# Pooled attention with a SwiGLU layer on one Trainium2 core: 68 instead of 30 products of zeros in the first tile

## The chip, the cores and the metric

The kernel runs on one core of one Trainium2 chip. The metric is the device time of one execution in microseconds (us); less is better. Before the change the median of three runs is 977.51 us (976.91 to 977.65).

## What is computed

```python
k_p = k.reshape(B, H, Sp, pool, D).mean(axis=3)        # B=8, H=8, S=576, D=64, pool=8, Sp=72
v_p = v.reshape(B, H, Sp, pool, D).mean(axis=3)
scores = scale * np.matmul(q, k_p.transpose(0, 1, 3, 2))
scores = scores - np.max(scores, axis=-1, keepdims=True)
attn = np.exp(scores)
attn = attn / (np.sum(attn, axis=-1, keepdims=True) + 1e-09)
attn_out = np.matmul(attn, v_p)
x = attn_out.transpose(0, 2, 1, 3).reshape(B * S, H * D)   # 4608 tokens x 512
g = x @ w_gate                                             # d_ff = 1536
silu = g * (1.0 / (1.0 + np.exp(-g)))
out = (silu * (x @ w_val)) @ w_out
```

## The kernel before, in words

The 4608 tokens are cut into nine tiles of 512. A tile is filled by pieces of up to 128 tokens, each of which goes through the attention, and then runs through twelve chunks of 128 hidden columns: a gate product and a value product on TensorE (`side`, L797 to L799, three f16 products for each of four blocks of x), a tanh on ScalarE, two products on VectorE, and an output product (`project`, L824, L830 and L831) that is added up in four PSUM banks `acc`.

The first tile has to do more: it loads and splits all the weights, and it makes the pooled keys and values of two batches. Its order of work is written out by hand in the string `ORDER`. `first_tile` (L907) walks it from left to right; each name is a job of the table `jobs` (L992) and a number, and each engine executes its instructions in the order in which the jobs issue them. The tiles behind it are in another loop and are not touched.

The names used below, with the number of a piece of tokens or a weight chunk or a step of the first tile:

- `H`, `P`, `T` take the weights of a piece of attention into two f16 halves (ScalarE L600, GpSimd L606) and turn them with a transposing DMA (`pt<-half`, SyncE L637); `Y` is its product with the values (TensorE L646 to L649, 16 products); `X` (ScalarE L669) and `Z` (VectorE L673) write the piece into the x of the tile.
- `Lw` loads a weight chunk; `c` (ScalarE L218), `b` (ScalarE L212), `d` (VectorE L222), `e` (ScalarE L233), `f` (TensorE L181 and L182, sums over the partitions), `g` (VectorE L187), `h`, `j` (ScalarE L248), `i`, `k` (VectorE L253) split it into halves.
- `G` and `V` are the gate and the value product of a step (for steps 0 to 5 half a tile, 256 tokens: 12 products each); `t` is its tanh (ScalarE L807), `u` and `v` its products (VectorE L810 and L815), `w` (ScalarE L969) and `y` (VectorE L973) its two halves, `O` the output product (12 products: L824 four times, L830 and L831 four times each).
- `ZERO` begins the four banks `acc` with a product of zeros each (L937). `D` with a number n issues n more products of zeros (L941), each of 512 columns, and adds them to the first bank:

```python
        def idle(n):
            for _ in range(n):
                nc.tensor.matmul(kept["acc"][0], zeros[:, :P], zeros, start=False, stop=False)
```

They add nothing to the result. Steps 0 to 2 work on the first 256 tokens (pieces 0 and 1), steps 3 to 5 on the others (pieces 2 and 3), so `G3` needs `X3` and `Z3`. `G1` writes the bank from which `u0` reads.

Of the kernel before, what the change touches and what calls it, by code (L numbers as in the profile page):

```python
# [37 lines left out]
Lk0 Lq0 Lk1 Lv2 Lv1 Lv0 Lq1 Lw0 Kp0 Kb0 Kp1 CZ Lw1 Lr0 Lu0 S0 Vp0 M0 Lq2 Vp2 E0 Na0 S1  # L38
a0 N0 b0 Vp1 Lq3 M1 Vm0 a1 Vo0 E1 Vs0 Kq0 R0 Vx0 H0 Vh0 Vq0 b1 Vg0 S2 Lr1 Na1 Lu2 P0 S3
Lq4 Vf0 M2 N1 T0 Lq5 H1 Kq1 Vq2 E2 c0 Y0 Lu1 Na2 X0 d0 Z0 Lw2 P1 l0 Vq1 e0 M3 T1 m0 f0  # L40
c1 N2 g0 ZERO Vm1 h0 Vo1 E3 d1 H2 j0 Vs1 Lw3 P2 e1 R1 D10 Y1 Vg1 Vx1 T2 a2 X1 l1 Vh1 un0
b2 m1 Z1 D8 f1 g1 k0 S4 i0 a3 G0 h1 Lq6 j1 M4 un1 c2 V0 k1 t0 Y2 E4 d2 b3 Lw4 i1 Na3 u0
l2 N3 D8 G1 v0 X2 w0 c3 y0 m2 Z2 O0 t1 d3 H3 V1 e2 u1 Lw5 P3 v1 l3 f2 g2 e3 T3 a4 h2 f3
j2 g3 un2 i2 w1 j3 y1 h3 k2 D4 O1 b4 i3 G2 k3 a5 V2 b5 t2 Y3 c4 u2 m3 X3 v2 Vf1 Z3 d4 G3
w2 c5 y2 Lw6 un3 t3 O2 l4 d5 e4 V3 u3 Lw7 m4 l5 f4 G4 v3 g4 w3 m5 y3 j4 O3 e5 k4 V4 Na4
t4 c6 u4 N4 f5 G5 v4 g5 h4 w4 a6 S5 H4 y4 t5 un5 b6 i4 V5 Lq7 u5 P4 M5 O4 G6 v5 T4 un4
a7 w5 c7 y5 d6 E5 O5 t6 j5 u6 Lw8 S6 e6 k5 Na5 V6 h5 Lq8 M6 l6 N5 H5 i5 f6 G7 v6 E6 P5
g6 w6 h6 y6 j6 T5 a8 O6 t7 u7 un6 Na6 c8 S7 b8 b7 V7 M7 i6 G8 E7 v7 d7 w7 Y4 y7 Lw9 N6
e7 O7 t8 d8 H6 X4 u8 Lw10 m6 Y5 e8 Z4 V8 l8 k6 X5 m8 l7 Z5 c9 f7 f8 v8 m7 G9 g7 w8 g8 j7
un7 y8 j8 un8 a9 h7 V9 t9 Na7 b9 u9 N7 O8 v9 i7 k7 w9 H7 y9 G10 k8 c10 d9 h8 V10 t10  # L50
Lw11 i8 e9 u10 La0 a10 l9 f9 O9 v10 m9 g9 w10 h9 y10 j9 un9 O10 i9 b10 k9 La1 a11 G11
b11 d10 V11 t11 Pa0 l10 u11 e10 G12 v11 w11 y11 c11 m10 f10 O11 g10 t12 d11 h10 j10 u12
l11 un10 V12 k10 e11 i10 m11 La2 G13 v12 P6 w12 y12 f11 O12 t13 g11 P7 T6 u13 h11 j11 T7
k11 S8 Ln i11 un11 Pa2 V13 M8 La3 E8 G14 La4 Na8 v13 N8 w13 y13 Y6 Pa3 t14 u14 V14 X6
Pa4 H8 La5 P8 O13 v14 La6 w14 T8 y14 Z6 Pa5 Y7 Pa6 Y8 X7 Z7 X8 La7 Pa1 Z8 Pa7 A A
"""
SIGN_AS_INT = (5, 8, 11)
TILE = 512
# [1085 lines left out]
```

## Time and profile before

| what | value |
|---|---|
| median of the runs | 977.51 us (976.91 to 977.65) |
| the profiled execution, its own time | 975.54 us |
| its span in the trace | 973.8 us |
| TensorE busy | 939.7 us, 97% of the span |
| VectorE, ScalarE, GpSimd busy | 566.0, 461.2, 241.3 us |
| mean granted clock of TensorE | 0.993 |
| products of zeros by `D` (L941) | 30 |

The span runs from the first to the last instruction of the trace; the time of the same execution is 1.74 us longer. "Busy" of TensorE counts the time in which a product is under way. The granted clock is 1.00 at 2.4 GHz and 0.50 at 1.2 GHz. A row of the timeline may hold several instructions of the same line (x8); the bracket behind it says how long the engine had been idle ahead of it, and what ended that.

### The profile page before, as it was taken

The page shows a single profiled execution, that of the slowest core. Times are in us where ns is not written, and L with a number is a line of the kernel's source. Part 1 is how long each engine was busy: PE and PEld are TensorE (multiplying, and loading weights), DVE is VectorE, ACT ScalarE, POOL GpSimd, SP SyncE. Part 2 cuts the span into 40 slices and gives each one's busy share as a digit, 9 for nine tenths or more (in the row PEclk, how much of TensorE's full clock was granted, in tenths as well). Part 3 has the DMA queues.
Part 4 walks back from the last instruction along what each step waited for, and adds up shares of the span by engine and source line. Part 5 has one row for each costly group of instructions (what it writes and reads, how often), then busy time and mean ns, then how long its engine had stood idle before and what let it go on. Part 6 is the DMA issues. An engine that isn't in the chain of part 4 may idle for free.

```text
span 973.8 us, 14306 instructions
## 1 busy us (share of the span) xinstructions
PE 939.7 (97%) x5486; PEld 498.4 (51%) x5486; DVE 566.0 (58%) x1005; ACT 461.2 (47%) x864; POOL 241.3 (25%) x327
## 2 busy tenths in 40 slices
PE   5779999799999999999999999999999999999998
PEld 4657545354555555554555555554545555444443
DVE  6788877667766675586446675674444454323222
ACT  3898883245554553544254544552454443222222
POOL 4533336035226230521025211620121201000000
PEclk9899999999999999999999999999999999999999
DMA  9855426246437342653047232840231222001001
GB/s 349 237 154 208 154 109 171 80 115 186 92 109 211 102 83 79 187 127 82 13 88 235 57 70 87 251 86 15 77 83 43 71 66 55 11 1 44 0 1 44
DMA packets 155524, 103.02 MB, mean 106 GB/s; under 512 B 113216, under 2 KB 141888, under 8 KB 153920
## 3 DMA queue, kind: packets, MB, share of 16 engines
q1 hardware_dynamic: 155456, 102.11, 37.3%
q8 instruction: 43, 0.70, 0.3%
q14 instruction: 25, 0.20, 0.1%
HBM read 67.63 MB, written 9.44 MB: 79 GB/s over the span
## 4 chain that ended last, share of the span: by engine, by line
PE 87%; DMA 6%; POOL 2%; ACT 2%; issue 1%; DVE 1%; SPq 0%; POOLq 0%; DVEq 0%; ACTq 0%
PE gv L797 18%; PE gv L798 18%; PE gv L799 18%; PE acc L824 10%; PE acc L830 9%; PE acc L831 9%; DMA pt<-half 2%; DMA kr<-k_rows 1%; DMA in<-v_rest 1%; DMA in<-k_rows 1%; PE ps L542 1%; PE ps L658 1%; PE ps L543 1%; PE ps L659 1%; DMA k<-k_rows 1%
## 5 line engine op out<-in xcount | busy, mean ns | idle before, releaser
L797 PE MATMUL gv<-x,wgv_h 128*128 128x512 f16 (+1 forms) x888 | 332.0, 374 | 3.8 <-ACT x L669 1.8
L798 PE MATMUL gv<-x,wgv_h 128*128 128x512 f16 (+1 forms) x888 | 331.8, 374 | 1.3 <-DVE x L673 1.3
L799 PE MATMUL gv<-x,wgv_l 128*128 128x512 f16 (+1 forms) x888 | 331.9, 374 | 0.5 <-DVE wgv_l L253 0.5
L810 DVE SCALAR_TENSOR_TENSOR hf<-hf,gv 128x512 f32<-128x512 f32 (+1 forms) x111 | 74.1, 668 | 171.6 <-ACT hf L807 171.3
L807 ACT ACTIVATE hf<-gv,un 128x512 f32<-128x512 f32 (+1 forms) x111 | 74.8, 674 | 193.9 <-PE gv L799 193.9
L1076 ACT CAST hh<-gv 128x512 fp32r<-128x512 f32 x96 | 56.3, 586 | 227.2 <-DVE gv L815 227.2
L831 PE MATMUL acc<-hb,wo_l 128*128 128x512 bf16 x384 | 145.5, 379 | 0.0
L824 PE MATMUL acc<-hh,wo_h 128*128 128x512 f32 (+1 forms) x444 | 139.5, 436 | 0.0
L799 PEld LDWEIGHTS <-wgv_l 128*128 128x128 f16 x888 | 87.0, 98 | 102.2 <-issue 1.7
L798 PEld LDWEIGHTS <-wgv_h 128*128 128x128 f16 x888 | 87.0, 98 | 98.1 <-issue 4.7
L797 PEld LDWEIGHTS <-wgv_h 128*128 128x128 f16 x888 | 87.4, 98 | 94.3
L1080 DVE TENSOR_TENSOR hl<-gv,hh 128x512 bf16<-128x512 f32 x96 | 66.3, 691 | 111.0 <-ACT hb L1077 111.0
L525 POOL TENSOR_TENSOR box<-qt,box 64x512 f16<-64x512 f32 (+1 forms) x60 | 64.0, 1067 | 227.8 <-issue 160.9
L815 DVE SCALAR_TENSOR_TENSOR gv<-gv,un,hf 128x512 f32<-128x512 f32 (+1 forms) x111 | 82.3, 741 | 63.0 <-PE gv L799 62.3
L830 PE MATMUL acc<-hl,wo_b 128*128 128x512 bf16 x288 | 109.8, 381 | 0.0
L824 PEld LDWEIGHTS acc<-hh,wo_h 128*128 128x128 f32 x444 | 83.2, 191 | 24.2 <-ACT hh L969 0.3
L630 POOL TENSOR_TENSOR half<-sc,half 128x512 f16<-128x512 f32 (+1 forms) x30 | 34.7, 1158 | 215.8 <-ACT half L620 193.6
L831 PEld LDWEIGHTS <-wo_l 128*128 128x128 bf16 x444 | 43.7, 98 | 37.9
L1077 ACT CAST hb<-gv 128x512 bf16<-128x512 f32 x96 | 56.8, 591 | 0.0
L830 PE MATMUL acc<-hl,wo_h 128*128 128x512 bf16 (+1 forms) x156 | 56.7, 368 | 0.0
L830 PEld LDWEIGHTS <-wo_b 128*128 128x128 bf16 x288 | 28.3, 98 | 42.2 <-issue 16.6
L523 ACT ACTIVATE qt<-qt,inv 128x512 f32<-128x512 f32 (+1 forms) x60 | 40.9, 682 | 0.0
(143 smaller groups left out, 1121.5 us busy)
## 6 DMA issues: line engine op xcount, KB each, us to landing
ws<-w_all SPq DMA_DIRECT2D x12, 1536.0 KB, 7.1
qt<-q_twice SPq DMA_DIRECT2D x48, 256.0 KB, 3.2
out_t<-ob SPq DMA_DIRECT2D x36, 256.0 KB, 2.3
in<-k_rows SPq DMA_DIRECT2D x12, 576.0 KB, 3.9
in<-q_rows SPq DMA_DIRECT2D x12, 576.0 KB, 5.2
in<-v_main SPq DMA_DIRECT2D x12, 512.0 KB, 4.3
in<-v_rest SPq DMA_DIRECT2D x12, 512.0 KB, 5.7
qt<-q_rows SPq DMA_DIRECT2D x8, 256.0 KB, 4.3
```

Source lines behind the costliest of these rows:

```text
L525: nc.gpsimd.tensor_sub(o[rows], qt[rows], o[rows])
L797: nc.tensor.matmul(o, wh, x["h"][:, j, a:e], start=(j == 0), stop=False)
L798: nc.tensor.matmul(o, wh, x["l"][:, j, a:e], start=False, stop=False)
L799: nc.tensor.matmul(o, wl, x["h"][:, j, a:e], start=False, stop=(j == NJ - 1))
L807: nc.scalar.activation(hf, gate, AF.Tanh, scale=un[:, c, 0:1])
L810: nc.vector.scalar_tensor_tensor(out=hf, in0=hf, scalar=1.0, in1=gate, op0=ALU.add, op1=ALU.mult)
L815: nc.vector.scalar_tensor_tensor(out=out, in0=val, scalar=un[:, c, 2:3], in1=hf, op0=ALU.mult, op1=ALU.mult)
L824: nc.tensor.matmul(o, wo_h[:, c, js], hh[:, :n], start=begin, stop=False)
L830: nc.tensor.matmul(o, wo[:, c, js], hl[:, :n], start=False, stop=False)
L831: nc.tensor.matmul(o, wo_l[:, c, js], hb[:, :n], start=False, stop=end)
L1077: nc.scalar.copy(hb[:, :n], val)
L1080: nc.vector.tensor_sub(hl[:, :n], val, hh[:, :n].bitcast(F32))
```

## The change

Only the string `ORDER` changes. The four `D` that stand there get larger or stay, and four are new. In the order of the program:

| place | before | after |
|---|---|---|
| ahead of `Y1` | 10 | 14 |
| behind `Y1`, ahead of `f1` | 8 | 9 |
| behind `Y2`, ahead of `G1` | 8 | 16 |
| behind `O0`, ahead of `V1` | none | 5 |
| behind `V1`, ahead of `f2` | none | 5 |
| between `f2` and `f3` | none | 6 |
| behind `f3`, ahead of `O1` | 4 | 4 |
| behind `O1`, ahead of `G2` | none | 9 |
| sum | 30 | 68 |

The core of the diff (the lines behind it are the same jobs, broken otherwise):

```diff
-c1 N2 g0 ZERO Vm1 h0 Vo1 E3 d1 H2 j0 Vs1 Lw3 P2 e1 R1 D10 Y1 Vg1 Vx1 T2 a2 X1 l1 Vh1 un0
-b2 m1 Z1 D8 f1 g1 k0 S4 i0 a3 G0 h1 Lq6 j1 M4 un1 c2 V0 k1 t0 Y2 E4 d2 b3 Lw4 i1 Na3 u0
-l2 N3 D8 G1 v0 X2 w0 c3 y0 m2 Z2 O0 t1 d3 H3 V1 e2 u1 Lw5 P3 v1 l3 f2 g2 e3 T3 a4 h2 f3
-j2 g3 un2 i2 w1 j3 y1 h3 k2 D4 O1 b4 i3 G2 k3 a5 V2 b5 t2 Y3 c4 u2 m3 X3 v2 Vf1 Z3 d4 G3
+c1 N2 g0 ZERO Vm1 h0 Vo1 E3 d1 H2 j0 Vs1 Lw3 P2 e1 R1 D14 Y1 Vg1 Vx1 T2 a2 X1 l1 Vh1 un0
+b2 m1 Z1 D9 f1 g1 k0 S4 i0 a3 G0 h1 Lq6 j1 M4 un1 c2 V0 k1 t0 Y2 E4 d2 b3 Lw4 i1 Na3 u0
+l2 N3 D16 G1 v0 X2 w0 c3 y0 m2 Z2 O0 t1 d3 H3 D5 V1 e2 u1 Lw5 P3 v1 l3 D5 f2 g2 e3 T3 a4
+h2 D6 f3 j2 g3 un2 i2 w1 j3 y1 h3 k2 D4 O1 b4 i3 D9 G2 k3 a5 V2 b5 t2 Y3 c4 u2 m3 X3 v2
+Vf1 Z3 d4 G3
```

On TensorE, behind `V1`, where the sums `f2` and `f3` (`ps<-least` and `ps<-wm`, the sums of two weight chunks) stand, the instructions were these; all line numbers of the changed kernel are one higher.

```order
L799 MATMUL gv_643<-x,wgv_l 128x256
L181 MATMUL ps<-least,ones 128x2
L182 MATMUL ps<-wm,ones 128x2
L181 MATMUL ps<-least,ones 128x2
L182 MATMUL ps<-wm,ones 128x2
L941 LDWEIGHTS zeros
L941 MATMUL acc_407<-zeros 128x512
```

And now at the same place:

```order
L800 MATMUL gv_661<-x,wgv_l 128x256
L942 LDWEIGHTS zeros
L942 MATMUL acc_407<-zeros 128x512
...
L182 MATMUL ps<-least,ones 128x2
L183 MATMUL ps<-wm,ones 128x2
L942 LDWEIGHTS zeros
L942 MATMUL acc_407<-zeros 128x512
...
L182 MATMUL ps<-least,ones 128x2
L183 MATMUL ps<-wm,ones 128x2
L942 LDWEIGHTS zeros
L942 MATMUL acc_407<-zeros 128x512
```

Five products of zeros now precede the first sum and six the second. On the other four engines and their queues every instruction stands where it stood.

## Rows read from the trace of the kernel before

**Rows 1.** The page, section 2: granted clock in 40 slices of the span.
```profile
PEclk9899999999999999999999999999999999999999
```

**Rows 2.** Windows: length, busy us of PE, PEld, DVE, ACT, POOL, clock, DMA, GB/s.
```profile
42.87:46.28 3.41, 3.41 (x21) 2.19 (x20) 1.54 (x3) 1.73 (x3) 0.46 (x1) 0.50 1.13 363
63.35:66.74 3.39, 3.39 (x13) 2.22 (x14) 2.94 (x7) 3.39 (x6) 1.87 (x3) 0.50 0.94 329
73.59:77.00 3.41, 3.41 (x18) 2.65 (x17) 3.22 (x3) 3.22 (x6) 0.34 (x1) 0.50 0.33 86
77.00:166.00 89.00, 88.85 (x555) 51.35 (x554) 71.12 (x117) 66.72 (x110) 40.51 (x51) 1.00 0.48 162
```

**Rows 3.** The chain that ended last, pieces in order of time (start, us, what).
```profile
34.02 8.66 DMA pt<-half
62.13 8.50 DMA pt<-half
143.09 0.24 PE ps L182 x2
```

**Rows 4.** Timeline of TensorE, first tile, from the zeros ahead of Y1.
```profile
37.69 2.32 PE L941 MATMUL acc<-zeros 128*128 128x512 f16 x10
...
42.73 0.23 PE L646 MATMUL ps<-pt,vst_h 128*128 128x128 f16 x1 [2.71 <-DMA pt<-half]
...
44.31 2.87 PE L941 MATMUL acc<-zeros 128*128 128x512 f16 x8
```

**Rows 5.** Timeline of ScalarE: X1, w0, X3, t3, the last instruction of e4.
```profile
44.55 0.69 ACT L669 ACTIVATE x<-ps,r 128x512 f16<-128x512 f32 x1 [1.90 <-PE ps L649]
...
57.16 0.35 ACT L969 CAST hh<-gv 128x256 fp32r<-128x256 f32 x1
...
71.77 0.69 ACT L669 ACTIVATE x<-ps,r 128x512 f16<-128x512 f32 x1 [0.57 <-PE ps L649]
...
75.60 0.48 ACT L807 ACTIVATE hf<-gv,un 128x256 f32<-128x256 f32 x1 [0.19 <-PE gv L799]
...
77.62 0.19 ACT L233 ACTIVATION_READ_ACCUMULATOR wgv_h<-wf 128x1 f32 x1
```

**Rows 6.** Timeline of VectorE: g1 and u0.
```profile
47.55 0.16 DVE L187 TENSOR_SCALAR p2w<-ps 128x2 uint32<-128x2 uint32 x1 [1.53 <-PE ps L182]
...
55.88 0.37 DVE L810 SCALAR_TENSOR_TENSOR hf<-hf,gv 128x256 f32<-128x256 f32 x1
```

**Rows 7.** Timeline of TensorE, from the zeros ahead of G1 to G4.
```profile
52.61 1.89 PE L941 MATMUL acc<-zeros 128*128 128x512 f16 x8
56.30 0.27 PE L797 MATMUL gv<-x,wgv_h 128*128 128x256 f16 x1 [1.80 <-ACT ws L212]
...
57.57 0.74 PE L824 MATMUL acc<-hh,wo_h 128*128 128x256 f32 x4
...
59.06 0.27 PE L797 MATMUL gv<-x,wgv_h 128*128 128x256 f16 x1
...
60.37 0.28 PE L181 MATMUL ps<-least,ones 128*128 128x2 f32 x2
61.48 0.38 PE L182 MATMUL ps<-wm,ones 128*128 128x2 f32 x2 [0.83 <-ACT wgv_h L233]
...
63.23 0.50 PE L182 MATMUL ps<-wm,ones 128*128 128x2 f32 x2 [1.14 <-ACT wgv_h L233]
63.59 1.87 PE L941 MATMUL acc<-zeros 128*128 128x512 f16 x4
...
67.33 0.27 PE L797 MATMUL gv<-x,wgv_h 128*128 128x256 f16 x1
...
70.67 0.22 PE L646 MATMUL ps<-pt,vst_h 128*128 128x128 f16 x1 [0.55 <-DMA pt<-half]
...
73.30 0.27 PE L798 MATMUL gv<-x,wgv_h 128*128 128x256 f16 x1 [0.52 <-DVE x L673]
...
78.95 0.36 PE L182 MATMUL ps<-wm,ones 128*128 128x2 f32 x2
```

More of the change, by code (lines that the diff above doesn't have):

```diff
@@ L40 @@
 Lq4 Vf0 M2 N1 T0 Lq5 H1 Kq1 Vq2 E2 c0 Y0 Lu1 Na2 X0 d0 Z0 Lw2 P1 l0 Vq1 e0 M3 T1 m0 f0
-c1 N2 g0 ZERO Vm1 h0 Vo1 E3 d1 H2 j0 Vs1 Lw3 P2 e1 R1 D10 Y1 Vg1 Vx1 T2 a2 X1 l1 Vh1 un0
-b2 m1 Z1 D8 f1 g1 k0 S4 i0 a3 G0 h1 Lq6 j1 M4 un1 c2 V0 k1 t0 Y2 E4 d2 b3 Lw4 i1 Na3 u0
-l2 N3 D8 G1 v0 X2 w0 c3 y0 m2 Z2 O0 t1 d3 H3 V1 e2 u1 Lw5 P3 v1 l3 f2 g2 e3 T3 a4 h2 f3
-j2 g3 un2 i2 w1 j3 y1 h3 k2 D4 O1 b4 i3 G2 k3 a5 V2 b5 t2 Y3 c4 u2 m3 X3 v2 Vf1 Z3 d4 G3
-w2 c5 y2 Lw6 un3 t3 O2 l4 d5 e4 V3 u3 Lw7 m4 l5 f4 G4 v3 g4 w3 m5 y3 j4 O3 e5 k4 V4 Na4
@@ L46 @@
[L46 to L55, printed above, removed]
+c1 N2 g0 ZERO Vm1 h0 Vo1 E3 d1 H2 j0 Vs1 Lw3 P2 e1 R1 D14 Y1 Vg1 Vx1 T2 a2 X1 l1 Vh1 un0
+b2 m1 Z1 D9 f1 g1 k0 S4 i0 a3 G0 h1 Lq6 j1 M4 un1 c2 V0 k1 t0 Y2 E4 d2 b3 Lw4 i1 Na3 u0
@@ new lines @@
+l2 N3 D16 G1 v0 X2 w0 c3 y0 m2 Z2 O0 t1 d3 H3 D5 V1 e2 u1 Lw5 P3 v1 l3 D5 f2 g2 e3 T3 a4
+h2 D6 f3 j2 g3 un2 i2 w1 j3 y1 h3 k2 D4 O1 b4 i3 D9 G2 k3 a5 V2 b5 t2 Y3 c4 u2 m3 X3 v2
+Vf1 Z3 d4 G3 w2 c5 y2 Lw6 un3 t3 O2 l4 d5 e4 V3 u3 Lw7 m4 l5 f4 G4 v3 g4 w3 m5 y3 j4 O3
+e5 k4 V4 Na4 t4 c6 u4 N4 f5 G5 v4 g5 h4 w4 a6 S5 H4 y4 t5 un5 b6 i4 V5 Lq7 u5 P4 M5 O4
+G6 v5 T4 un4 a7 w5 c7 y5 d6 E5 O5 t6 j5 u6 Lw8 S6 e6 k5 Na5 V6 h5 Lq8 M6 l6 N5 H5 i5 f6
+G7 v6 E6 P5 g6 w6 h6 y6 j6 T5 a8 O6 t7 u7 un6 Na6 c8 S7 b8 b7 V7 M7 i6 G8 E7 v7 d7 w7 Y4
@@ new lines @@
+y7 Lw9 N6 e7 O7 t8 d8 H6 X4 u8 Lw10 m6 Y5 e8 Z4 V8 l8 k6 X5 m8 l7 Z5 c9 f7 f8 v8 m7 G9
+g7 w8 g8 j7 un7 y8 j8 un8 a9 h7 V9 t9 Na7 b9 u9 N7 O8 v9 i7 k7 w9 H7 y9 G10 k8 c10 d9 h8
+V10 t10 Lw11 i8 e9 u10 La0 a10 l9 f9 O9 v10 m9 g9 w10 h9 y10 j9 un9 O10 i9 b10 k9 La1
+a11 G11 b11 d10 V11 t11 Pa0 l10 u11 e10 G12 v11 w11 y11 c11 m10 f10 O11 g10 t12 d11 h10
+j10 u12 l11 un10 V12 k10 e11 i10 m11 La2 G13 v12 P6 w12 y12 f11 O12 t13 g11 P7 T6 u13
+h11 j11 T7 k11 S8 Ln i11 un11 Pa2 V13 M8 La3 E8 G14 La4 Na8 v13 N8 w13 y13 Y6 Pa3 t14
@@ L56 @@
+u14 V14 X6 Pa4 H8 La5 P8 O13 v14 La6 w14 T8 y14 Z6 Pa5 Y7 Pa6 Y8 X7 Z7 X8 La7 Pa1 Z8 Pa7
+A A
 """
```

## The prediction

> **What bounds the kernel now.** I read the slices of the granted clock first: only the second of 40, from 24 to 49 us, is below 9 tenths [rows 1], so whatever the zeros do for the clock is decided early. The windows give the falls exactly. From 42.87 to 46.28, 63.35 to 66.74 and 73.59 to 77.00 us TensorE is at 0.50 (1.2 GHz), busy without a break; from 77 to 166 us it is at 1.00 and busy 88.85 of 89.00 us [rows 2]. A fourth stretch lies ahead of the first changed place and is left as it is. Ahead of each of the three the engine stood idle: 2.71 us ahead of Y1; 0.83 and 1.14 us at f2 and f3; 0.55, then the waits for X3 and Z3, of which the last was 0.52 us [rows 4, 7].
>
> Then the chain: which of these falls costs time? It runs through the transposing DMA that lands at 42.68 and the one from 62.13 to 70.63 us, and turns into TensorE only after that; at 143.09 it still goes through a weight sum of TensorE [rows 3]. So what happens ahead of 70.67 us counts only through what makes that DMA start, or if TensorE reaches Y3 later than the DMA lands; what happens behind it counts nearly in full. The DMA from 62.13 waits for P3, this for H3 on ScalarE, and from X1 at 44.55 us ScalarE has no wait until 71.2 us (X3 at 71.77 shows the first, 0.57) [rows 5]. ScalarE is therefore what sets the DMA's start, and X1 waited 1.90 us for TensorE's Y1.
>
> One bound holds for all of this: about 0.2% (1.95 us) is what a measurement of this kernel can tell from no change. A half-speed stretch of 3.41 us costs 1.70 us of TensorE work at most.
>
> **The change part by part.** One product of zeros at 2.4 GHz takes 0.216 us, since ten take 2.32 and eight 1.89 us [rows 4, 7]. That makes 38 more = 8.2 us of TensorE; the question is what they lie in.
>
> *D10 to D14.* Four more end 0.86 us later, at 40.87 instead of 40.01, in a wait that ends at 42.73 with the DMA [rows 4]. They cost nothing; the idle stretch shrinks from 2.71 to 1.85 us. Is that enough for the clock? The nearest row on the one side is this place, where the clock fell behind 2.71 us; the nearest on the other is G1, where it stayed at 1.00 behind eight products of zeros and 1.80 us of idle time [rows 7]. 1.85 is close to the second, so I take it that the fall at 42.87 goes. If it does, Y1 takes as long as Y3: 70.67 to 71.77, 1.10 us, against 42.73 to 44.55, 1.82 us [rows 4, 5, 7]. X1 and all of ScalarE behind it come 0.72 us earlier, so P3, and with it the DMA that now starts at 62.13: it would land at 69.9. (On SyncE's queue it stands behind weight loads, which wait for ScalarE's wf of an earlier chunk and so move with it.) If the fall stays, this term is nothing.
>
> *D8 to D9.* At full clock Y1's 16 products are issued by 43.65 and nine products end at 45.6; now eight end at 47.02 [rows 4]. f1 and g1 come 1.4 us earlier (g1 waited 1.53 us for it [rows 6]). VectorE then reaches u0 1.3 us earlier, at 54.6, bounded by ScalarE's wf (c2).
>
> *D8 to D16.* G1 starts when u0 has left its bank: u0 runs from 55.88 for 0.37 us, and G1 starts at 56.30 [rows 6, 7]. (The row names ScalarE, which ended at the same moment.) With 1.4 us gained, sixteen products run from 51.2 to 54.6 us, and G1 can start at about 55.0. The eight more lie in the wait, and cost nothing. O0 waits for w0 on ScalarE, 57.16 + 0.35 [rows 5], 0.72 earlier: 56.86.
>
> *D5, D5, D6, D9.* From O0 on there is hardly a wait left to fill. The work up to Y3 at full clock: O0 1.49 (57.57 to 59.06), V1 1.31 (59.06 to 60.37), two sums at 0.36 as at 78.95, 5 + 5 + 6 + 4 + 9 = 29 products of zeros 6.26, O1 1.49 as O0, G2 and V2 2.62 as twice V1 [rows 7]: 13.9 us. So TensorE comes to Y3 at 56.86 + 13.9 = 70.75 us, 0.08 later than now and 0.8 us later than the DMA. What the early ScalarE gains, these 25 products give back. The sum holds at full clock, which I take as the 20 products around f2 and f3 lie in the two waits (0.83 and 1.14) that precede the fall at 63.35.
>
> *The fall at 73.59.* With D9 TensorE works through from O1 to the end of Y3; the 0.55 us ahead of Y3 are gone, and only the waits for X3 and Z3 are left. The idle time there is at most 1.53 us (X3's start at 71.77 to 73.30 [rows 5, 7]), less than the 1.80 us that G1 stood without harm, so I take it that the clock stays. Behind 73.3 TensorE is what others wait for, so up to 1.70 us come back. ScalarE lets only part of that through: t3 waited just 0.19 us for G3, and f4 on TensorE (78.95) needs e4, whose last instruction ends at 77.81 [rows 5, 7]. With Y3 0.08 late, e4 ends no earlier than 77.7, so f4 can start at 77.8 to 77.9: some 1.0 us gained. Behind 77 us the engine is busy without a break [rows 2], and what follows moves with it.
>
> *Sum.* 0 + 0 + 0 + 0.08 - 1.1 = about -1.0 us, so the profiled execution would take 974.5 instead of 975.54 us. The median of the runs is 1.97 us above that execution; I put the same step on it: **976.5 us**. Between the bounds: if nothing is late at Y3 and ScalarE follows, -0.72 - 1.70 = -2.4; if no clock is gained at all, +2.7 (below).
>
> **The rivals.**
>
> 1. *The gain comes through in full.* The DMA at 69.9 sets Y3, the fall at 73.59 goes, and ScalarE, 0.72 us earlier, follows: -2.4, 975.1 us. For it: two falls did lie on the chain. Against it: my 13.9 us behind O0. It needs one of the terms there to be 0.8 us too long.
>
> 2. *The fall at 42.87 stays.* 1.85 us of idle time is still more than 1.80. Then X1 is as now, the nine products end at 47.2, u0 0.2 us later, G1 at 56.5, O0 at 57.8 and Y3 at 71.7, 1.0 late; the fall at 73.59 is gone, and ScalarE, which starts from the late X3, gives back little over the 1.0: -0.1, 977.4 us, no change.
>
> 3. *The falls lie elsewhere in other executions.* All of the gain hangs on the fall at 73.59, ahead of which the idle stretches (0.55 us and at most 1.53) are shorter than at the other two places; in an execution without it the same edits bring +0.08: 977.6 us. The three runs lie within 0.74 us, less than one such fall, which speaks against much change from one to the next. The Trainium skill (TensorE: Matmul & The Clock Gate, What's actually happening) says that one kernel shows different numbers of products at the lower level from run to run; no row of one profiled execution can show that. By that rule the time is this rival's.
>
> 4. *The other side: products of zeros do not hold the clock, and 25 of them stand on TensorE's path to Y3.* Ten in a row ended at 40.01 and the clock fell 2.9 us later all the same; the four at 63.59 ran at half speed [rows 2, 4, 7]. Then all falls stay: O0 at 57.8, 13.9 us of work and 1.7 us for the fall at 63.35 put Y3 at 73.4, 2.7 late, with the fall behind it unchanged: 980.2 us. It decides from the point where the clock falls near 63 us although 15 products stand ahead of it. Against it: the row at 52.61, where eight products and a wait of 1.80 brought no fall.
>
> That the change doesn't issue what it says is excluded by the order of TensorE above; the other engines' order is the same.
>
> **How the numbers follow.** Forecast 0.40 (976.5 us), rival 1 0.22, rival 2 0.14, rival 3 0.14, rival 4 0.10. Faster by over 0.2% means below 975.55: rival 1 and a trifle of the forecast, 0.23. Slower means above 979.46: rival 4, 0.10. The rest, 0.67, is no difference. The range leaves out rival 4 and the ends of the others: from 974.6 (rival 1 and half a microsecond, about the spread of the three runs) to 978.6 (rival 2 with Y3 1.0 late and nothing given back).
>
> **What would show it.** In the profile after: an idle stretch of about 1.85 us ahead of Y1, and no 0.50 behind it; X1 at 43.8; G1 near 55.0 right behind sixteen products; the transposing DMA issued near 61.4; no wait ahead of Y3, which starts near 70.75; clock 1.00 from 63 to 77 us; f4's last product near 77.9. Wrong would be: a wait of TensorE for the DMA at Y3 (then rival 1), a fall behind 42.9 (2), any fall between 63 and 77 (4), or a first tile that is 1 us shorter with the gap around 166 to 185 us that much longer.

## The result, and the profile after

The changed kernel takes 981.02 us at the median (977.68 to 982.17, five runs), the kernel before 977.51 us (976.16 to 979.72, five runs in the same session). The ratio is 1.0041 with a 95% interval of [1.0023, 1.0058]: slower by 0.4%. (The ratio is estimated from all the runs; it is not the quotient of the two medians, which is 1.0036.) I had put 976.5 us and a range up to 978.6. The profiled execution of the change takes 981.02 us, with a span of 979.2.

The windows of the profile after come first, cut at the first product of `D14` (42.45 us) and at G3's second product, the one that waits for Z3 (77.64 us). Columns as in [rows 2].

```profile
24.66:28.07 3.41, 3.41 (x20) 3.19 (x20) 2.80 (x8) 3.37 (x6) 1.91 (x3) 0.51 0.57 186
34.85:41.70 6.85, 5.19 (x23) 4.64 (x24) 3.59 (x9) 3.62 (x7) 2.38 (x2) 0.50 0.92 292
0.00:42.45 42.45, 27.01 (x193) 24.79 (x193) 25.61 (x60) 20.59 (x28) 19.97 (x34) 0.88 0.84 287
42.45:77.64 35.19, 31.16 (x244) 21.07 (x244) 28.47 (x54) 32.67 (x50) 11.75 (x16) 1.00 0.64 166
77.64:979.20 901.56, 888.25 (x5091) 456.39 (x5090) 513.17 (x893) 408.66 (x789) 210.44 (x277) 1.00 0.34 94
77.00:166.00 89.00, 86.20 (x539) 50.28 (x538) 70.78 (x116) 68.33 (x112) 36.01 (x44) 1.00 0.46 155
```

The same three pieces of the kernel before, cut at its `D10` and its G3:

```profile
0.00:37.69 37.69, 23.52 (x192) 21.78 (x193) 25.12 (x60) 19.92 (x28) 19.63 (x34) 0.95 0.87 303
37.69:73.30 35.61, 26.79 (x205) 19.24 (x205) 28.20 (x54) 32.40 (x51) 11.31 (x16) 0.90 0.72 186
73.30:973.80 900.50, 889.39 (x5091) 457.34 (x5090) 512.64 (x893) 408.90 (x789) 210.32 (x277) 1.00 0.34 94
```

This is not what a median of +3.5 us suggests. Most of the difference between these two executions, 4.76 us, lies ahead of the first changed place, in instructions that are the same: in the one after, the clock was at 0.50 from 24.7 and again from 34.9 us. The piece that the change touches is 0.42 us shorter. It runs at 1.00 throughout, where before it ran at 0.90. But the piece behind it is 1.06 us longer, although before spent 3.4 us of it at half clock and after none as long as TensorE had work (its next fall begins at 976.9 us, behind the last product). From 77 to 166 us TensorE is busy 86.20 us instead of the 88.85 of [rows 2]: 0.52 us of that is still the wait for Z3, but the rest is new, it has begun to wait.

Two profiles can therefore not give the cause. They do show where the changed piece works, on TensorE (the answer to [rows 4, 7]):

```profile
42.45 3.18 PE L942 MATMUL acc<-zeros 128*128 128x512 f16 x14
45.47 0.22 PE L647 MATMUL ps<-pt,vst_h 128*128 128x128 f16 x1
...
46.38 2.11 PE L942 MATMUL acc<-zeros 128*128 128x512 f16 x9
...
55.09 3.62 PE L942 MATMUL acc<-zeros 128*128 128x512 f16 x16
59.40 0.27 PE L798 MATMUL gv<-x,wgv_h 128*128 128x256 f16 x1 [0.69 <-DVE hf L811]
60.62 0.72 PE L825 MATMUL acc<-hh,wo_h 128*128 128x256 f32 x4
62.08 1.24 PE L942 MATMUL acc<-zeros 128*128 128x512 f16 x5
64.47 1.24 PE L942 MATMUL acc<-zeros 128*128 128x512 f16 x5
...
65.91 1.46 PE L942 MATMUL acc<-zeros 128*128 128x512 f16 x6
...
69.55 0.27 PE L831 MATMUL acc<-hl,wo_h 128*128 128x256 bf16 x1 [0.49 <-DVE hl L974]
70.44 2.10 PE L942 MATMUL acc<-zeros 128*128 128x512 f16 x9
75.00 0.22 PE L647 MATMUL ps<-pt,vst_h 128*128 128x128 f16 x1
```

The fourteen products began so late that they ended only at 45.63 us; the DMA for Y1 had landed at 44.52, so Y1 starts 0.95 us behind it. The sixteen products leave 0.69 us of the wait ahead of G1. From O0 (60.62) to Y3 (75.00) are 14.38 us; before it was 13.10, a fall of the clock, two waits for weight sums and the wait for the DMA included [rows 7]. The waits at f2, f3 and Y3 are gone. The transposing DMA for Y3 is issued at 65.09, and the view of its tile gives

```profile
L638 SPq DMA_TRANSPOSE pt<-half x1: 2599/2599/2599, 65.1 to 65.1; - x1
DMA to landing us min/median/max: 7.0/7.0/7.0
```

so it lands at 72.1, and Y3 starts 2.9 us later. Before, Y3 started 0.04 us after the landing [rows 3, 7].

The chain of the profile after, in order of time, shows what hangs on that:

```profile
76.11 0.70 ACT x L670
...
76.83 0.75 DVE x L674
77.58 1.68 DVE wf L223
...
79.31 7.36 DMA ws<-w_all
...
86.76 0.19 ACT wf L219
```

X3 and Z3 follow Y3; on VectorE the `d` of a weight chunk (L223) stands behind Z3, and the next weight load waits for it, lands 7.36 us later and holds up ScalarE. TensorE feels it twice:

```profile
89.79 0.27 PE L798 MATMUL gv<-x,wgv_h 128*128 128x256 f16 x1 [0.72 <-DVE hl L974]
...
124.32 0.38 PE L798 MATMUL gv<-x,wgv_h 128*128 128x512 f16 x1 [1.32 <-DVE hl L974]
```

The kernel before has neither wait.

### The profile page after: what moved, and what is told of

The parts are those of the page before. It is cut to its first block, busy times and chain, and to the rows that moved or that the text cites. A ratio compares the mean times of both kernels' runs of the same rounds, so it can differ in the third digit from the quotient of the medians.

```text
span 979.2 us, 14382 instructions
## 1 busy us (share of the span) xinstructions
PE 946.4 (97%) x5524; PEld 502.3 (51%) x5524; DVE 567.3 (58%) x1005; ACT 461.9 (47%) x864; POOL 242.2 (25%) x327
## 4 chain that ended last, share of the span: by engine, by line
PE 84%; DMA 6%; DVE 4%; ACT 2%; issue 2%; POOL 1%; SPq 0%; ACTq 0%; DVEq 0%; POOLq 0%
PE gv L798 17%; PE gv L799 17%; PE gv L800 17%; PE acc L825 9%; PE acc L831 9%; PE acc L832 9%; DMA ws<-w_all 2%; PE ps L382 1%; DMA in<-k_rows 1%; DMA v<-v_main 1%; PE ps L659 1%; PE ps L543 1%; PE ps L544 1%; PE ps L660 1%; DVE wf L223 1%
```

## The experiments

**Theory A:** the products between O0 and Y3 stand on TensorE's path; what their waits don't take up delays Y3, and with it the weight loads. **Theory B:** the time was lost ahead of the change by chance, and the change costs nothing. **Theory C:** the three places up to G1 cost. Each kernel was timed beside the kernel before, whose median in the three sessions was 977.06, 976.99 and 977.13 us (97 runs, 973.48 to 984.18); the "clock" is the mean of the granted clocks of a kernel's timed runs, 0.992 for the kernel before in each session.

**The change again.** No edit.

> The changed kernel once more. Theory A (the 25 new products between O0 and Y3 stand on TensorE's path, so Y3 starts 3 us after its DMA has landed): 980 to 982 us at the median again, and in the profile Y3 starts 1.5 us or more after the DMA has landed. Theory B (the time was lost ahead of the first changed place, by falls of the clock that differ from execution to execution, and the change itself costs nothing): the first product of D14 starts anywhere from 37 to 43 us, and the median of five comes back to within 1.5 us of the kernel before. Theory C (the products ahead of G1 cost it): G1 starts right behind the sixteen products, without a wait.

978.91 us, ratio 1.0023 [1.0009, 1.0038], clock 0.9961 (0.9934 in the first five runs). Slower again, though by less than in the first five runs, and below the 980 that A wanted. In its profile Y3 starts at 74.88, 2.8 us after its DMA, as A says. Of B's two signs one came: `D14` starts at 42.83, inside its range, and the beginning was slow again; the median of the twelve runs is 1.85 us above before, a little more than B's bound. C asked for G1 behind the sixteen products without a wait; it waited 0.46 us.

**The first three places alone,** and once more.

```diff
-... O0 t1 d3 H3 D5 V1 e2 u1 Lw5 P3 v1 l3 D5 f2 g2 e3 T3 a4 h2 D6 f3 ... D4 O1 b4 i3 D9 G2
+... O0 t1 d3 H3 V1 e2 u1 Lw5 P3 v1 l3 f2 g2 e3 T3 a4 h2 f3 ... D4 O1 b4 i3 G2
```

> Only the first three places are raised (14, 9 and 16), the four new ones are left out. Theory A: no slower than before, 975.5 to 978 us, and Y3 waits for its DMA. Theory B: like the kernel before and like the changed kernel, all within their scatter. Theory C: as slow as the changed kernel, 980 to 982 us.

> Only the first three places raised, once more. Theory A: no slower than before, 975.5 to 977.5 us, with a mean clock above that of before by 0.001 to 0.003. If these three cost as well and the first time was luck: 978 us or more.

976.27 us, 0.9993 [0.9975, 1.0011], and 978.12 us, 1.0007 [0.9988, 1.0025]; clock 0.9938 and 0.9923. Neither interval excludes no difference. The second median lies outside A's range and just inside that for "luck" (978 us or more), and its clock did not rise as A wanted. C falls: 13 more products ahead of Y1, f1 and G1 cost nothing that can be measured (0.25% at most, the upper end of the second interval). They bring nothing either. The profile of the first timing begins as before did, its zeros starting at 37.66 us instead of 37.69, and shows one reason:

```profile
37.66 3.18 PE L941 MATMUL acc<-zeros 128*128 128x512 f16 x14
42.99 0.23 PE L646 MATMUL ps<-pt,vst_h 128*128 128x128 f16 x1 [2.15 <-DMA pt<-half]
```

```profile
43.30:46.70 3.40, 3.40 (x20) 2.03 (x18) 1.25 (x3) 1.99 (x3) 0.72 (x1) 0.50 1.12 328
```

The wait ahead of Y1 shrank to 2.15 us and the clock fell all the same, at 43.3 us; X1 starts at 44.71, no earlier than before. One sign of A failed here: Y3 does not wait for its DMA but comes 0.81 and 0.83 us behind it, without any of the new products. So a late Y3 alone is no sign of them; what they add is the difference in length. From O0 to Y3 these two profiles take 12.31 and 12.32 us, the two of the change 14.38 and 14.41; from O0 to G3's second product 14.94 and 15.04 against 17.02 and 17.04.

**The four new places alone.**

```diff
-e1 R1 D14 Y1 ... Z1 D9 f1 ... N3 D16 G1
+e1 R1 D10 Y1 ... Z1 D8 f1 ... N3 D8 G1
```

> The first three places stay at 10, 8 and 8, and the four new ones (5, 5, 6, 9) are added. Theory A: as slow as the changed kernel or slower, 980 to 983 us, with Y3 later than its DMA by 1.5 us or more. Theory B: within scatter of the kernel before. Theory C: like the kernel before, 976.5 to 978.5 us.

980.90 us, 1.0035 [1.0019, 1.0051], clock 0.9926; Y3 starts 1.8 us after its DMA. The loss is here, as A says, and B falls: with the same beginning and the same chances, this part is slower and the other is not. From O0 to G3's second product its profile takes 17.04 us, 2.0 to 2.1 us more than with the first three places alone and 1.3 more than the profile of before (15.73). The loss is 3.4 us, with an interval from 1.9 to 5.0; whether there is more to it than this path is not shown.

**The change without the nine behind O1, and the two halves of the new places alone.**

```diff
-... D4 O1 b4 i3 D9 G2
+... D4 O1 b4 i3 G2
```

> The changed kernel without the nine products behind O1. Theory A: up to 1.9 us of the loss come back (9 x 0.216), 978.5 to 980 us, and Y3 starts nearer to the DMA's landing. Theories B and C: as the changed kernel.

> The kernel before with the nine products behind O1 alone. Theory A (what stands between O0 and Y3 delays Y3 by as much as no wait takes up): the wait ahead of Y3 in the profile of before was 0.55 us, so 1.94 - 0.55 = 1.4 us are added and one fall less gives back 1.2: 977 to 979 us, 0 to 2 us over before, and Y3 starts 1 us or more after its DMA has landed. If the nine keep the clock and that decides: 975 to 976.5 us. If they are as dear as the 18 more were (6 to 8 us for 18): 980 to 981 us.

> The kernel before with the 5, 5 and 6 products between O0 and f3 alone. Theory A: 3.45 us of work, of which the two waits (0.83 and 1.14) take up at most 1.97: 1.5 us are added and about one fall less gives back 1.2, so 976.5 to 979 us. If the sums f2 and f3, which they delay, hold up ScalarE and the weight chunks as well: 979 to 981 us. Together with the nine alone it should come to the 3.4 us that the four new places cost.

Without the nine: 977.57 us, 1.0008 [0.9988, 1.0027], better than A's 978.5 to 980; Y3 starts 1.0 us after its DMA, nearer to it, as A says; B and C, which asked for the time of the changed kernel, miss. The nine alone: 978.38 us, 1.0018 [0.9999, 1.0037], inside A's range. The 5, 5 and 6 alone: 980.03 us, 1.0023 [1.0007, 1.0038], beyond A's 979 and inside the 979 to 981 set for the case that the delayed sums f2 and f3 hold up ScalarE as well; the interval reaches from 977.8 to 980.8 and cannot tell the two apart. The profile shows that case: ahead of the `h` behind f2 ScalarE, which has no wait there before [rows 5], stands

```profile
67.02 1.34 ACT L248 ACTIVATE wgv_h<-wf,sw 128x512 f16<-128x512 f32 x2 [1.45 <-DVE sw L190]
```

and G3 then waits 1.32 us for X3 instead of 0.78. (A fall of the clock at 59.0 us may have a part in it.) The halves add up to 0.41%, the four places together measured 0.35%. Which half is dearer stays open: the intervals overlap. The profile of the nine alone shows A's mechanism once more:

```profile
66.28 2.19 PE L941 MATMUL acc<-zeros 128*128 128x512 f16 x9
70.92 0.22 PE L646 MATMUL ps<-pt,vst_h 128*128 128x128 f16 x1
```

The DMA had landed at 69.34; TensorE came 1.6 us later.

**Eighteen more behind O1.**

```diff
-... D4 O1 b4 i3 D9 G2
+... D4 O1 b4 i3 D27 G2
```

> The changed kernel with 27 instead of 9 products behind O1, 18 more. Theory A (what stands between O0 and Y3 is on the path): all of it is added, 18 x 0.216 = 3.9 us over the changed kernel, 983 to 985 us. Theory B (the change itself costs nothing, the beginning scatters): as the changed kernel within the scatter, 977 to 981 us. A third one, that Y3's DMA sets the path and the products fill waits, gives under 1 us.

987.40 us, 1.0104 [1.0083, 1.0124], clock 0.9933. More than A's 983 to 985. Its profile and that of the kernel without the nine happen to reach O0 at the same time, so they can be laid beside each other. With 27:

```profile
56.17 0.74 PE L824 MATMUL acc<-hh,wo_h 128*128 128x256 f32 x4 [0.40 <-ACT hh L969]
...
66.01 5.99 PE L941 MATMUL acc<-zeros 128*128 128x512 f16 x27
74.46 0.22 PE L646 MATMUL ps<-pt,vst_h 128*128 128x128 f16 x1
...
77.09 0.27 PE L798 MATMUL gv<-x,wgv_h 128*128 128x256 f16 x1 [0.52 <-DVE x L673]
```

With none there:

```profile
56.21 0.74 PE L824 MATMUL acc<-hh,wo_h 128*128 128x256 f32 x4 [0.40 <-ACT hh L969]
...
68.70 0.22 PE L646 MATMUL ps<-pt,vst_h 128*128 128x128 f16 x1
...
71.86 0.27 PE L798 MATMUL gv<-x,wgv_h 128*128 128x256 f16 x1 [0.52 <-DVE x L673]
```

27 products of 0.216 us are 5.83 us; Y3 is 5.76 later, so nothing hides them up to there, and G3's second product is 5.23 later, since with none there G3 waits longer for X3 (1.31 us instead of 0.78). The next weight loads are issued at 78.77 instead of 73.54 us, 5.23 later too. That the median rose by 6.4 to 8.5 us for 18 products (3.9 us) is more than the path up to G3 explains; the rest lies behind G3 (903.7 against 900.4 us to the end in these two profiles, which are of the fastest of six and the second fastest of twelve executions) and was not taken apart.

**No product of zeros by `D`.**

```diff
-e1 R1 D14 Y1 ... Z1 D9 f1 ... N3 D16 G1
+e1 R1 Y1 ... Z1 f1 ... N3 G1
```

(and the other five `D` left out likewise)

> No product of zeros by D at all. If the products hold the clock and that is worth time, slower than before by 1 to 3 us, 978 to 980 us, with a mean clock below the 0.992 of before. If the falls they prevent lie beside waits, no slower, 976 to 978 us: the clock falls more often and the time does not follow.

980.07 us, 1.0034 [1.0020, 1.0049], clock 0.9857. So the 30 products of before are worth 3 us. That they do it by the clock is what its drop from 0.992 says. Without them TensorE stands 4.42 us ahead of Y1, and the rows of Y1 are those of half clock:

```profile
42.13 0.29 PE L646 MATMUL ps<-pt,vst_h 128*128 128x128 f16 x1 [4.42 <-DMA pt<-half]
42.21 0.31 PE L647 MATMUL ps<-pt,vst_h 128*128 128x128 f16 x1
```

**Three versions that were to be faster:** as many products as the waits at f2 and f3 hold; products in the waits of the first 35 us; products between Y3 and G3. All have the first three places of the change.

```diff
-... l3 f2 g2 ... h2 f3 ... k2 D4 O1
+... l3 D3 f2 g2 ... h2 D5 f3 ... k2 O1
```

> The first three places as in the change (14, 9, 16); ahead of f2 three, between f2 and f3 five, and none elsewhere, so that about as many stand there as the two waits (0.83 and 1.14 us) hold, and Y3 is not later than before. Theory A: as fast as with the first three places alone or a little faster, 975 to 977 us. Theory B: within the scatter of before. If any product ahead of Y3 costs its 0.216 us: 1 us slower than with the first three places alone.

```diff
+        def early(n):
+            if "early" not in kept:
+                kept["early"] = gv_bank(1, TILE)
+            for _ in range(n):
+                nc.tensor.matmul(kept["early"], zeros[:, :P], zeros, start=True, stop=True)
...
-Vq0 ... Vq2 ... Vq1
+W5 Vq0 ... W5 Vq2 ... W4 Vq1
```

> The first three places as in the change, and 14 products of zeros in the three waits of TensorE between 20 and 35 us (into a bank that is idle then), where the profiles show falls ahead of every changed place. If those early falls set the path (the changed kernel's profile was 4.4 us late at 40 us), faster than with the first three places alone by 1 to 2 us, 974 to 975.5 us, and the scatter shrinks. If DMA landings set it, the same as those, 976 to 977 us. If the 14 products delay what is behind them: 977 to 979 us.

```diff
-Vf1 Z3 d4 G3
+Vf1 Z3 d4 D3 G3
```

> The first three places as in the change, and three products of zeros between Y3 and G3, in the wait of 0.78 us for X3, where they delay nothing. If a fall behind 73 us is what is left to gain: 974.5 to 976 us, below the first three places alone, and no fall between 70 and 80 us in the profile. If not: as the first three places alone, 976 to 977 us.

The first: 980.00 us, 1.0035 [1.0014, 1.0056], clock 0.9914; an outright miss. Y3 is on time (0.04 us after its DMA), and O0 to G3 takes 15.02 us, as with the first three places alone, yet the kernel is slower: A doesn't explain this one. Without the four products ahead of O1 TensorE waits 1.10 us there for w1, and its clock falls at 74.9 and for 6.8 us at 419.6 us; how much each cost isn't settled. The second: 977.85 us, 1.0001 [0.9986, 1.0016], with the clock up to 0.9949 and no gain; the median lies in the range for a delay by the 14 products, the interval includes no difference. The third: 979.14 us, 1.0022 [1.0005, 1.0039], clock 0.9911, a miss; its profile has two falls far behind and none between 70 and 80 us, but neither have those of the first three places alone, so that shows nothing of the three products. No version here beats the kernel before.

## Why the prediction was wrong

**The three places up to G1: right in the time.** They were put at nothing, and cost nothing that two timings could tell. But the reason given, that the fall at 42.87 goes and X1 comes 0.72 us earlier, holds in some executions only. The clock fell at 43.3 us behind 2.15 us of idle time in the profile of the first three places alone, and did not fall behind 1.94 us in that without the nine. In the profile after the zeros began so late that Y1 stood behind them. G1 there waits 0.69 us behind sixteen products, where 0.4 were forecast.

**"What the early ScalarE gains, these 25 products give back": the failed step.** I put Y3 at 0.08 us later than before and 0.8 us later than its DMA. In the two profiles of the change it is 2.9 and 2.8 us later than its DMA. Two sizes were off. The DMA took 7.0 us, not the 8.5 of the one execution that I had, and so landed earlier against TensorE. And O0 to Y3 took 14.38 us instead of 13.9, because O1 waits 0.49 us for hl, which the sum of busy times left out. In 11 of the 14 profiles this DMA took 6.8 to 7.3 us. And 0.08 us was the distance to a Y3 that this long DMA had held up, behind a fall of the clock at 63.35: the forecast compared the products with a late Y3. Beside the profiles of before and of the first three places alone they put G3 off by 1.3 to 2.1 us, and the four places together were measured at 0.35%, 3.4 us.

**"The fall at 73.59 goes, some 1.0 us gained": wrong.** It was a fall of that one execution. In the 14 profiles of these kernels a fall begins between 72 and 76 us in three. And where the clock stayed at 1.00, as after, nothing of it came back: the piece behind G3 was 1.06 us longer. My sentence that "what follows moves with it" overlooked a queue: the weight load behind `d` behind Z3. It is late when Y3 is late, and in the profile after TensorE waits for what hangs on it (0.72 and 1.32 us). That these waits make the loss is not shown: such a pair of over 0.5 us each stands in three of the 14 profiles only, in which this load took 7.36, 8.09 and 7.14 us; in the others it took 6.3 to 6.7, that of the four new places alone among them, which is as slow without these waits.

**The clock did rise:** from 0.992 to 0.9934 and 0.9961 in the timed runs, which is 13 and 8 us at half clock instead of 16 (twice the missing share of 977 us). The change does what its form suggests: in the 14 profiles a fall begins between 63.0 and 65.4 us in each of the seven that have no products around f2 and f3, and in none of the seven that have some. But it pays more for it than it returns. At the same mean clock, 0.996, the kernel before took 973.5 to 973.7 us (three executions) and the changed one 977.7 to 978.9 (four).

**The rivals.** The first, Y3 set by its DMA, is seen in neither profile of the change; the second, a fall behind D14 all the same, is what the first three places alone showed. The third, that the falls lie elsewhere in other executions, was right in its premise: with the first three places alone the clock fell at 29.6, 43.3 and 63.7 us in one profile and at 23.2, 33.4 (for 6.8 us) and 64.1 in the other. The Trainium skill (TensorE: Matmul & The Clock Gate, What's actually happening) has the same kernel run a different number of products at the lower level from run to run; the traces agree: 61 and 56 products are recorded in these stretches, 10.2 and 13.6 us long. The third rival's price, +0.08 us, had the same missing term as the forecast. I had argued against it from three runs within 0.74 us; 97 runs spread over 10.7. The fourth had the right side, "25 of them stand on TensorE's path to Y3", and the wrong reason: the products do hold the clock, and from 41.7 us on it never fell in the first 80. A longer path to Y3 does not need a lost clock; whether that path makes all of the 3.4 us stays open.

## What to carry to other kernels

A filler instruction is free only while the engine behind it would have waited anyway, and the wait must be measured in more than one execution: the same place waited 0.55 us for its DMA in one profile and 0.19 in another, and in the other twelve TensorE was the late one, by 0.8 to 6.9 us, in five of them without any of the new products ahead of it. Ask what else is queued behind the delayed step on other engines; here a weight load hung on it. And the time at half clock is no measure of what is lost: with products in the first 35 us and up to G1 the mean clock rose to 0.9949, and no change of the time could be measured. The chain of the kernel before goes through a DMA there, from 34.02 to 42.68 us [rows 3]; that this is the reason was not tried.

## What was not expected of the hardware

The first 40 us scatter by 6 us in instructions that are the same in all kernels but the one with early products: the first product of the first `D` starts at 36.88 us in the profile without the nine, at 37.66 in that of the first three places, at 40.02 in that of the four new places alone and at 42.83 in that of the change run again, and it is late where the clock fell at 24 to 28 and near 35 us. Far behind the change, between 417 and 423 us, TensorE waits for VectorE's `sc`: 0.55 us before, 1.47 after, and in the profile of the first three places

```profile
418.79 0.21 PE L658 MATMUL ps<-box,pt 128*128 128x64 f16 x1 [2.46 <-DVE sc L553]
```

with the clock at 0.50 behind it. Six of the 14 profiles have a fall there. What sets the length of that wait was not tried; it may add to the scatter of every kernel here, and a part of the misses above may be its doing.
